# GpSimd's layer-norm rows written as multiply and add, with a newly searched order of the work

## The chip, the cores and the metric

The kernel runs on one core of a Trainium2 chip. The metric is device time in microseconds (us) of one execution; a kernel's time is the median of several runs. The engines are called as in the profile: PE (TensorE matmul), PEld (its weight loads), DVE (VectorE), ACT (ScalarE), POOL (GpSimd) and SP (SyncE, which here only issues DMAs).

## What is computed

One sequence of 2048 rows of width 448 passes through an attention block with 16 heads of width 28 that share one K and one V, and then through a block in which only 8 selected rows take part:

```python
def _layernorm(x, eps=1e-5):
    return (x - mean(x)) / sqrt(var(x) + eps)

def _A_ref(x, wq, wk, wv, wo):             # S=2048, D=448, H=16, Dh=28
    q = (x @ wq) by heads;  k = x @ wk;  v = x @ wv
    p = softmax(q @ k.T * Dh ** -0.5)      # 16 heads x 2048 x 2048
    return (p @ v, heads side by side) @ wo

def _B_ref(x, w_r, w_gate, w_up, w_down):
    r = x @ w_r;  idx = the 8 rows of largest r
    y = (silu(x[idx] @ w_gate) * (x[idx] @ w_up)) @ w_down * sigmoid(r[idx])
    return x, with y added to the rows idx

h  = x + _A_ref(_layernorm(x), wq, wk, wv, wo)
h2 = h + _B_ref(_layernorm(h), w_r, w_gate, w_up, w_down)
```

## The kernel before

**Tiles.** The rows are cut into 16 tiles of 128 (`NT`). Attention goes by 16 blocks of queries (index b, 128 queries of all heads) and in each by 16 tiles of keys (index j). A pair (b, j) is one unit of softmax work, 128 keys against 2048 query columns: PE makes the scores (L804 or L810), another engine makes the exponentials, and PE adds their product with V to one bank of PSUM (L830), which DVE empties at the end of the block (L892).

**Two ways to an exponential.** In 175 of the 256 pairs ACT computes it, in two instructions of 128x1024 each (L846, 350 in all). In the other 81 (`_ND` says how many in each block) DVE turns the scores into the bit pattern of a bf16 power of two, in four instructions (L858, tile `Y0`), and two shifted copies of it are made (`Y1`, and a third, `Y2`), which are weighted together by three products with V. The copy `Y2` is always made by POOL in one instruction of 128x2048 (L874). The copy `Y1` is made either by POOL with L874 again or by DVE in pieces of 128x1536 (L868). `_GK` decides that for three pairs at a time: 1 means POOL, 0 means DVE. With 81 pairs its first 27 entries count.

**The ramp.** Before any of that, a row tile has to be normalised, transposed and projected. `group(g)` (L697) does it for groups of tiles: 0, 1, (2,3), (4,5), (6,7), (8 to 11), (12 to 15). In a group DVE takes mean and variance (L702, L704). For groups 0 to 2 ACT makes the reciprocal deviation (L707, L709); for the four groups from 3 on POOL does it: variance plus epsilon (L712), then the power -0.5 (L714, in tile `rstd`). The normalised rows `of` are then made by DVE for tile 0 (L721), by ACT for tiles 1 and 2 (L726), and by POOL for the 13 tiles 3 to 15, with the row mean subtracted and the result multiplied by `rstd` (L730). PE transposes them (L741), DVE copies the transposes into `xnT` (L746), PE projects them to K and V (L615, a helper for many matmuls), and DVE writes K (L756) and Vs (L765). A key tile can be used by the softmax once its K and V stand. `q_project` makes the queries of a block (DVE, L786).

**After the blocks.** `evict` divides by the softmax's sum with the help of small DMAs and a multiplication on POOL (L901); `out_proj` projects, takes the second layer norm (POOL makes a power of it, L926) and stores the rows; `tail` selects the 8 rows and passes them through the second block.

**The order of the work.** Nothing is ordered by hand. Each instruction is entered with a planned duration and a priority (the third argument of `G.op`, and `prio`), and `_Flow.plan` (L316) simulates the engines with these durations and writes down, for each engine, a fixed order. The chip then runs each engine's list strictly in that order, with semaphores for the dependencies. So a wrong planned duration doesn't change what is computed; it makes an order that was meant for another timing. The priorities are offset by a table `_W` by kind of work (A and D: scores for ACT and for DVE, C: L858, S: L868, P and V: products with V, G: the groups, Q: `q_project`, O: `out_proj`), and further constants steer the planner (`_WIN`, `_HOLD`, `_LATE`, `_LOOK`). Planned durations that the text comes back to: 685 ns for L730, 100 ns for L712, 690 ns for L714, 1976 ns for L874 (`_SHIFT`).

Of the kernel before, what the change touches and what calls it, by code (L numbers as in the profile page):

```python
# [7 lines left out]
ALU = mybir.AluOpType  # L8
AX = mybir.AxisListType
F32 = mybir.dt.float32  # L10
# [6 lines left out]
PE, AC, DV, PO, SP = "pe", "act", "dve", "pool", "sp"  # L17
# [7 lines left out]
class _Graph:  # L25
# [208 lines left out]
_STEP = (0, 43, 85)  # L234
_GAIN = 1.57769262
_NP = 8
_GK = (1, 0, 0, 1, 0, 1, 0, 1, 1, 0, 1, 0, 1, 0, 1, 0, 1, 1, 0, 1, 1, 0, 1, 0, 0, 1, 0, 1, 1, 0, 0, 0, 1, 0, 1, 1,
    1, 1, 1, 1)
_ND = (3, 4, 8, 3, 5, 6, 6, 5, 4, 7, 5, 4, 7, 4, 4, 6)
_W = {"A": -13.681, "D": -10.289, "C": -1.28, "S": 2.404, "P": 0.728, "V": -0.715, "G": -3.802, "Q": -12.936, "O":  # L240
    -29.732, "K": 1.19, "E": -0.647, "F": -0.883, "L": 1.034}
_SHIFT = 1976
_LOOK = 14405.4
_WIN = {PE: 155.3, AC: 3448.9, DV: 40.7, PO: 221.1, SP: 1.0}
_LATE = (2, 40.5)
_MOST = {"A": 1, "D": 2, "M": 3, "T": 9}
_TUNE = {}
_HOLD = {"A": 0.0, "D": 281.9}
_LOW = 0
_NEXT = 12.0  # L250

# [249 lines left out]
def _fast(nc, G, sb, ps, psb, flag, scr, rows, A_x, A_wq, A_wk, A_wv, A_wo, B_w_r, B_w_gate, B_w_up, B_w_down, out):  # L501
    S, D, H = A_x.shape[1], A_x.shape[2], 16
    DH = D // H
    FF = B_w_gate.shape[1]
    NT, CK = S // 128, 112
# [8 lines left out]
    EPS = 1e-5  # L514
# [8 lines left out]
    x_sb = sb("x_sb", [128, NT, D], BF16)  # L523
    of = sb("of", [128, NT, RW], BF16)
    bn6 = sb("bn6", [128, NT, 6], F32)
    mv = sb("mv", [128, NT, 2], F32)
    rstd = sb("rstd", [128, NT], F32)
    nb = sb("nb", [128, NT], F32)
    var = sb("var", [128, NT], F32)
    nhalf = sb("nhalf", [128, 4], F32)  # L530
    xnT = sb("xnT", [128, NCH, S], BF16)
# [13 lines left out]
    Q = sb("Q", [128, 3, 4, 128], BF16)  # L545
    K = sb("K", [128, 2, S], BF16)
    Vs = sb("Vs", [128, NC, NT, 32], BF16)
    P = sb("P", [128, NP, 2, 2, 512], BF16)
# [65 lines left out]
    def mm(o, l, r, start, stop):  # L614
        return lambda e: e.matmul(o() if callable(o) else o, lhsT=l, rhs=r, start=start, stop=stop)  # L615

    def bank(u, p=slice(0, 128), c=slice(0, 512), t=None):
        return lambda: (ps if t is None else t)[p, u.b[0], c]
# [32 lines left out]
    for g in range(2, len(loads)):  # L651
# [3 lines left out]
         writes=["ident"])  # L655
# [6 lines left out]
         writes=["pq0"])  # L662
    G.op(DV, lambda e: e.tensor_single_scalar(pq[:, 1:2], pidx[:, :], 32, ALU.bitwise_and), 62, reads=["pidx"],
         writes=["pq1"])
    G.op(DV, lambda e: e.tensor_scalar(kcol[:, 0:1], pq[:, 1:2], 0, KSCALE, ALU.is_equal, ALU.mult), 62, reads=["pq1"],
         writes=["k0"])
    G.op(DV, lambda e: e.tensor_scalar(kcol[:, 1:2], pq[:, 1:2], 32, KSCALE, ALU.is_equal, ALU.mult), 62,
         reads=["pq1"], writes=["k1"])
    G.op(DV, lambda e: e.tensor_scalar(kcol[:, 4:5], pq[:, 0:1], DH, ZERO / KSCALE, ALU.is_equal, ALU.mult), 62,
         reads=["pq0"], writes=["k4"])  # L670
    for r in range(2):
        G.op(DV, lambda e, r=r: e.tensor_scalar(kcol[:, 2 + r:3 + r], kcol[:, r:r + 1], kcol[:, 4:5], None, ALU.mult), 62,
             reads=["k%d" % r, "k4"], writes=["kb%d" % r])
    G.op(DV, lambda e: e.tensor_single_scalar(qone[:, :], pq[:, 0:1], DH, ALU.is_ge), 62, reads=["pq0"],
         writes=["qone"])
# [6 lines left out]
    for r in range(4):  # L682
        G.op(AC, lambda e, r=r: e.activation(wk_rep[0:CK, :, 32 * r:32 * r + DH], wk_sb[0:CK, :, :], ACT.Identity), 140,
             reads=["wk_sb"], writes=[("wkr", r)], after=[G.last_w["wk_rep"][0]])
# [12 lines left out]
    def group(g):  # L697
        tl_ = groups[g]
        n, t0, t1 = len(tl_), tl_[0], tl_[-1] + 1
        G.prio = (-3000, -2990, -2980)[g] if g < 3 else t0 / 16.0 + W["G"]  # L700
        for t in tl_:
            G.op(DV, lambda e, t=t: e.bn_stats(bn6[:, t, :], x_sb[:, t, :]), 516, reads=[("x", t)], writes=[("bn6", t)],  # L702
                 after=[G.last_w[("xnT", 0)][0]] if t == 2 else [G.last_w[("nb", 3)][0]] if t in (4, 5) else (), prio=-3001 if g == 2 else None)
            G.op(DV, lambda e, t=t: e.bn_aggr(mv[:, t, :], bn6[:, t, :]), 89, reads=[("bn6", t)], writes=[("mv", t)],  # L704
                 prio=-3001 if g == 2 else None)
        if g < XA:
            G.op(AC, lambda e: e.activation(var[:, t0:t1], mv[:, t0:t1, 1], ACT.Ln, bias=ebias[:, 0:1]), 200,  # L707
                 reads=[("mv", t) for t in tl_] + ["ebias"], writes=[("var", g)])
            G.op(AC, lambda e: e.activation(rstd[:, t0:t1], var[:, t0:t1], ACT.Exp, scale=-0.5), 200, reads=[("var", g)],  # L709
                 writes=[("rstd", g)])  # L710
        else:
            G.op(PO, lambda e: e.tensor_scalar(var[:, t0:t1], mv[:, t0:t1, 1], EPS, None, ALU.add), 100,  # L712
                 reads=[("mv", t) for t in tl_], writes=[("var", g)])
            G.op(PO, lambda e: e.tensor_tensor(rstd[:, t0:t1], var[:, t0:t1], nhalf[:, 0:n], ALU.pow), 690,  # L714
                 reads=[("var", g), "nhalf"], writes=[("rstd", g)])
        if 0 < g < XA:
            G.op(DV, lambda e: e.scalar_tensor_tensor(nb[:, t0:t1], mv[:, t0:t1, 0], -1.0, rstd[:, t0:t1], ALU.mult, ALU.mult), 70,
                 reads=[("rstd", g)] + [("mv", t) for t in tl_], writes=[("nb", t) for t in tl_], prio=-3002 if g == 2 else None)
        for t in tl_:
            if g == 0:  # L720
                G.op(DV, lambda e, t=t: e.tensor_scalar(  # L721
                    of[:, t, :].rearrange("p (a b) -> p a b", a=2)[:, :, 0:D // 2], x_sb[:, t, :],
                    mv[:, t, 0:1], rstd[:, t:t + 1], ALU.subtract, ALU.mult), 420,
                     reads=[("x", t), ("mv", t), ("rstd", g)], writes=[("of", t)])
            elif g < XA and t < 3:
                G.op(AC, lambda e, t=t: e.activation(of[:, t, 0:D], x_sb[:, t, :], ACT.Identity, bias=nb[:, t:t + 1],  # L726
                                                     scale=rstd[:, t:t + 1]), 640,
                     reads=[("x", t), ("nb", t), ("rstd", g)], writes=[("of", t)])
            else:
                G.op(PO, lambda e, t=t: e.tensor_scalar(of[:, t, 0:D], x_sb[:, t, :], mv[:, t, 0:1], rstd[:, t:t + 1],  # L730
                                                        ALU.subtract, ALU.mult), 685,
                     reads=[("x", t), ("mv", t), ("rstd", g)], writes=[("of", t)])
        for a in range(t0, t1, 2):
            m = min(2, t1 - a)
            u = G.unit()

            def cut(a, ch):
                return 2 * (ch // 2) if a == 0 else 0

            def tr(k, ch, u=u, a=a, m=m):  # L740
                return lambda e: e.transpose(psb[0:CK, u.b[0], (ch * m + k) * 128:(ch * m + k + 1) * 128],  # L741
                                             of[:, a + k, ch * CK + cut(a, ch):(ch + 1) * CK + cut(a, ch)], ident[:, :])
            G.op(PE, [tr(k, ch) for k in range(m) for ch in range(NCH)], m * 4 * (150 if g == 0 else 80),
                 reads=[("of", a + k) for k in range(m)] + ["ident"], writes=[u.key], take=u)
            dst = xnT[0:CK, :, a * 128:(a + m) * 128]
            G.op(DV, lambda e, u=u, m=m, dst=dst: e.tensor_copy(  # L746
                dst, psb[0:CK, u.b[0], 0:NCH * m * 128].rearrange("p (c n) -> p c n", c=NCH)), 65 + m * 265,
                 reads=[u.key], writes=[("xnT", a + k) for k in range(m)], free=u)
        sl = slice(t0 * 128, t1 * 128)
        w = n * 128  # L750
        uk = G.unit()
        G.op(PE, [mm(bank(uk, c=slice(0, w)), wk_rep[0:CK, ch, :], xnT[0:CK, ch, sl], ch == 0, ch == NCH - 1)
                  for ch in range(NCH)], 4 * (145 if g == 0 else 5 + w / 2.4), reads=[("wkr", r) for r in range(4)] + ["wk_rep"] + [("xnT", t) for t in tl_],
             writes=[uk.key], take=uk)
        for r in range(2):
            G.op(DV, lambda e, r=r: e.tensor_scalar(K[:, r, sl], ps[:, uk.b[0], 0:w], kcol[:, r:r + 1],  # L756
                                                        kcol[:, 2 + r:3 + r], ALU.mult, ALU.add), 190 + w * 1.04,
                     reads=[uk.key, "k%d" % r, "kb%d" % r], writes=[("K", r, t) for t in tl_], free=uk)
        if g == 0:
            q_project(0)  # L760
        uv = G.unit()
        G.op(PE, [mm(bank(uv, c=slice(32 * k, 32 * k + DH)), xnT[0:CK, ch, (t0 + k) * 128:(t0 + k + 1) * 128], wv_sb[0:CK, ch, :],
                     ch == 0, ch == NCH - 1) for k in range(n) for ch in range(NCH)], n * 4 * 55,
             reads=["wv_sb"] + [("xnT", t) for t in tl_], writes=[uv.key], take=uv)
        G.op(DV, lambda e: e.tensor_tensor(  # L765
            Vs[:, :, t0:t1, 1:1 + DH],
            ps[:, uv.b[0], 0:n * 32].rearrange("p (t c) -> p t c", c=32)[:, :, 0:DH].unsqueeze(1).broadcast_to([128, NC, n, DH]),
            vco[:, :, :].unsqueeze(2).broadcast_to([128, NC, n, DH]), ALU.mult), 65 + NC * n * 29,
            reads=[uv.key, "Vs0"] + ["vco%d" % v for v in range(NC)], writes=[("V", t) for t in tl_], free=uv)
# [906 lines left out]
def bass_sequential_preLN__grouped_kv_mqa__moe_arch_mod__prompt_kernel(  # L1676
# [3 lines left out]
    with es:  # L1680
# [11 lines left out]
        def build(cls, fn, pre, *args):  # L1692
# [6 lines left out]
            return g  # L1699

        G = build(_Flow, _fast, "")
        R = build(_Graph, _exact, "x_", G)

# [53 lines left out]
```

## Time and profile before

The median of three runs is 376.84 us (375.97 to 377.87). One execution was profiled; its own time was 377.56 us, of which 375.6 us are the span from its first to its last instruction and about 2 us lie around it.

| stretch of the profiled execution | what happens there |
|---|---|
| 0 to 10 us | loads, constants, tiles 0 and 1 |
| 10 to 49 us | the ramp: tiles 2 to 15 are normalised and projected, while ACT already works on the first pairs |
| 49 to 355 us | softmax on ACT, DVE and POOL together, PE between them |
| 355 to 376 us | last block's projection, selection of 8 rows, second block, scatter |

Over the span PE is busy for 89%, DVE for 90%, ACT for 89% and POOL for 80%. A row of the groups names line, engine, operation and tiles, then the count, the busy time in us, the mean duration in ns, and the idle time of that engine right ahead of it with what ended it. A row of the chain gives start and length in us. A row of the stretches gives the length, then busy time with the number of instructions of each engine, then the clock that PE was granted (1.00 is full), and the DMAs.

### The profile page before, as it was taken

The page shows a single profiled execution, that of the slowest core. Times are in us where ns is not written, and L with a number is a line of the kernel's source. Part 1 is how long each engine was busy: PE and PEld are TensorE (multiplying, and loading weights), DVE is VectorE, ACT ScalarE, POOL GpSimd, SP SyncE. Part 2 cuts the span into 40 slices and gives each one's busy share as a digit, 9 for nine tenths or more (in the row PEclk, how much of TensorE's full clock was granted, in tenths as well). Part 3 has the DMA queues.
Part 4 walks back from the last instruction along what each step waited for, and adds up shares of the span by engine and source line. Part 5 has one row for each costly group of instructions (what it writes and reads, how often), then busy time and mean ns, then how long its engine had stood idle before and what let it go on. Part 6 is the DMA issues. An engine that isn't in the chain of part 4 may idle for free.

```text
span 375.6 us, 8343 instructions
## 1 busy us (share of the span) xinstructions
PE 334.1 (89%) x3417; PEld 110.6 (29%) x3417; DVE 339.8 (90%) x693; ACT 334.7 (89%) x379; POOL 301.4 (80%) x211
## 2 busy tenths in 40 slices
PE   3786798999898999989998999999999989999985
PEld 3432322132323232322232232323232322222234
DVE  7763499899999897999999999999999999999984
ACT  5655399799999999999999999999999999999850
POOL 7799549569949899889789996999999997769701
PEclk9966699799999899999999999999999999999996
DMA  7661000010100010101000010000011060011100
GB/s 189 169 240 46 2 1 2 3 32 25 31 28 29 3 44 13 55 15 45 1 27 31 13 45 27 29 28 31 7 52 35 23 198 31 14 43 29 41 25 9
DMA packets 17974, 16.08 MB, mean 43 GB/s; under 512 B 6303, under 2 KB 15039, under 8 KB 17931
## 3 DMA queue, kind: packets, MB, share of 16 engines
q1 hardware_dynamic: 16426, 14.93, 12.9%
q8 instruction: 28, 0.46, 0.5%
q10 hardware_dynamic: 1392, 0.45, 0.5%
q0 software_dynamic: 112, 0.12, 0.1%
q14 instruction: 16, 0.12, 0.1%
HBM read 11.78 MB, written 3.71 MB: 41 GB/s over the span
## 4 chain that ended last, share of the span: by engine, by line
ACT 65%; DVE 14%; POOL 9%; PE 6%; DMA 3%; issue 1%; POOLq 0%; ACTq 0%; DVEq 0%
ACT P L846 65%; DVE Y L858 6%; POOL of L730 6%; PE ps L615 2%; PE ps L804 2%; DMA Rb<-l_scr 1%; DMA wqx<-in_A_wq_dram 1%; DVE Y L868 1%; PE ps L830 1%; POOL Y L874 1%; POOL rstd L714 1%; DMA l_scr<-Rc 1%; PE ps L741 1%; POOL On L901 1%; DVE junk L932 0%
## 5 line engine op out<-in xcount | busy, mean ns | idle before, releaser
L846 ACT ACTIVATE P<-ps 128x1024 bf16<-128x1024 f32 x350 | 323.3, 1227 | 21.9 <-PE ps L804 19.3
L874 POOL TENSOR_SCALAR Y<-Y 128x2048 int16<-128x2048 int16 x123 | 233.4, 1897 | 41.9 <-DVE Y L858 33.1
L858 DVE TENSOR_SCALAR Y<-ps 128x512 int16<-128x512 f32 x324 | 204.6, 678 | 7.5 <-PE ps L810 4.1
L804 PE MATMUL ps<-Q,K 32*128 32x512 bf16 (+1 forms) x700 | 139.3, 396 | 16.3 <-ACT P L846 13.8
L810 PE MATMUL ps<-Q,K 32*128 32x512 bf16 x324 | 102.6, 388 | 0.2 <-DVE Y L858 0.2
L830 PE MATMUL ps<-Y,Vs 128*32 128x512 bf16 x972 | 87.1, 393 | 1.7 <-DVE Ot L892 0.4
L804 PEld LDWEIGHTS ps<-Q,K 32*128 32x128 bf16 (+1 forms) x700 | 33.1, 92 | 138.5 <-ACT P L846 120.0
L830 PE MATMUL ps<-P,Vs 128*32 128x512 bf16 x700 | 62.4, 391 | 0.1
L868 DVE TENSOR_SCALAR Y<-Y 128x1536 int16<-128x1536 int16 x52 | 48.2, 936 | 0.1
L830 PEld LDWEIGHTS ps<-Y,Vs 128*32 128x32 bf16 x972 | 20.6, 93 | 42.5 <-issue 22.9
L810 PEld LDWEIGHTS ps<-Q,K 32*128 32x128 bf16 x324 | 24.8, 91 | 7.4 <-DVE Y L858 3.6
L730 POOL TENSOR_SCALAR of<-x_sb,mv,rstd 128x448 bf16<-128x448 bf16 x13 | 24.1, 1865 | 1.1 <-ACT rstd L709 0.7
L615 PE MATMUL ps<-xnT,wqx 112*128 112x128 bf16 x256 | 23.2, 232 | 0.4 <-DVE Y L858 0.2
L901 POOL TENSOR_TENSOR On<-Ot,Rb 128x512 bf16<-128x512 f32 x15 | 19.1, 1272 | 4.3 <-DMA Rb<-l_scr 3.3
L741 PE MATMUL ps<-ident,of 128*112 128x128 bf16 x64 | 8.1, 294 | 14.5 <-POOL of L730 9.2
L830 PEld LDWEIGHTS ps<-P,Vs 128*32 128x32 bf16 x700 | 14.5, 94 | 20.8 <-issue 20.0
L615 PE MATMUL ps<-wo_pad,On 128*128 128x448 bf16 x64 | 18.8, 363 | 0.5 <-DVE On L1063 0.3
L615 PEld LDWEIGHTS ps<-xnT,wqx 112*128 112x128 bf16 x256 | 15.9, 103 | 9.8 <-issue 5.7
L746 DVE COPY xnT<-ps 112x1024 bf16<-112x1024 bf16 (+1 forms) x9 | 5.7, 629 | 10.8 <-PE ps L741 10.6
L926 POOL TENSOR_TENSOR st<-st,nhalf 128x1 f32<-128x1 f32 x15 | 8.3, 552 | 5.8 <-DVE st L924 5.3
L756 DVE TENSOR_SCALAR K<-ps,kcol 128x256 bf16<-128x256 f32 (+2 forms) x14 | 7.4, 573 | 5.9 <-PE ps L615 5.8
L786 DVE TENSOR_SCALAR Q<-ps,qone 128x512 bf16<-128x512 f32 (+1 forms) x16 | 11.5, 721 | 0.7 <-PE ps L615 0.7
(162 smaller groups left out, 178.7 us busy)
## 6 DMA issues: line engine op xcount, KB each, us to landing
Rb<-l_scr SPq DMA_DIRECT2D x15, 256.0 KB
out_dram<-of SPq DMA_DIRECT2D x16, 112.0 KB, 2.3
n_rows<-of SPq DMA_DIRECT2D x14, 113.0 KB, 2.2
xnT<-in_B_w_down_dram SPq DMA_DIRECT2D x1, 1568.0 KB, 6.9
x_sb<-in_A_x_dram SPq DMA_DIRECT2D x3, 448.0 KB, 4.2
wg_sb<-in_B_w_gate_dram SPq DMA_DIRECT2D x1, 1344.0 KB, 8.4
wu_sb<-in_B_w_up_dram SPq DMA_DIRECT2D x1, 1344.0 KB, 6.7
wqx<-in_A_wq_dram ACTq DMA_DIRECT2D x1, 392.0 KB, 4.5
```

The lines of the kernel that those rows point to most:

```text
L615: return lambda e: e.matmul(o() if callable(o) else o, lhsT=l, rhs=r, start=start, stop=stop)
L730: G.op(PO, lambda e, t=t: e.tensor_scalar(of[:, t, 0:D], x_sb[:, t, :], mv[:, t, 0:1], rstd[:, t:t + 1], ALU.subtract, ALU.mult), 685, rea ...
L741: return lambda e: e.transpose(psb[0:CK, u.b[0], (ch * m + k) * 128:(ch * m + k + 1) * 128], of[:, a + k, ch * CK + cut(a, ch):(ch + 1) * ...
L786: G.op(DV, lambda e, c=c, src=src: e.tensor_scalar(Q[:, b % 3, c[0]:c[1], :], src(), qone[:, 0:1], None, ALU.add), 60 + n * 150, reads=[u. ...
L804: return e.matmul(ps[:, u.b[q], :], lhsT=K[a:a + w, r, j * 128:(j + 1) * 128], rhs=Q[a:a + w, b % 3, :, :].rearrange("p h n -> p (h n)"), ...
L810: return e.matmul(ps[:, u.b[0], :], lhsT=K[a:a + 32, u.i() % 2, j * 128:(j + 1) * 128], rhs=Q[a:a + 32, b % 3, :, :].rearrange("p h n -> p ...
L830: return e.matmul(ps[32 * i:32 * i + 32, ACC, :], lhsT=Vs[:, v, j, :], rhs=src(i), start=info["first"] == o.idx, stop=info["last"] == o.idx)
L846: G.op(AC, lambda e, u=u: e.activation(P[:, sl, u.r(), :, :], two(u), ACT.Exp, bias=EB, scale=OCT), 916, reads=[("U", "A", b, j, k)], writ ...
L858: G.op(DV, lambda e, u=u, g0=g0: e.tensor_scalar(Y0[:, g0, :].bitcast(I16), ps[:, u.b[0], :], 0.0, TOP - STEP[-1], ALU.max, ALU.min), 599, ...
L868: G.op(DV, lambda e, a12=a12, w=w: e.tensor_scalar(Y1[:, a12:a12 + w, 0:512].bitcast(I16), Y0[:, a12:a12 + w, :].rearrange("p a b -> p (a ...
L874: G.op(PO, lambda e, k=k, yk=yk: e.tensor_scalar(yk.bitcast(I16), Y0[:, 4 * s:4 * s + 4, :].bitcast(I16), 1.0, float(STEP[k]), ALU.mult, A ...
L901: G.op(PO, lambda e: e.tensor_tensor(On[:, rb, :, :].rearrange("p h n -> p (h n)"), Ot[:, rb, :], Rb[:, rb, :], ALU.mult), 1353, reads=[(" ...
```

## The change

POOL's normalised rows are computed as x times `rstd` plus a bias, in place of x minus mean, times `rstd`. The bias `nb` is the negated mean times `rstd`. The negated mean (`nmu`, a new tile) is made by DVE, in one instruction for each of the groups from 3 on; POOL multiplies it by `rstd`. The sum of variance and epsilon goes from POOL to DVE. Tile 3 belongs to group 2, whose bias was already made by DVE (L717) for tile 2; POOL's instruction for tile 3 now reads it. The planned duration of the power becomes 440 + 150 n ns for n tiles; that of the normalised row stays 685 ns. The planner's constants are replaced, and in `_GK` entry 24 goes from 0 to 1 (the other entries that differ are past the 27 that count).

```diff
-_GK = (1, 0, 0, 1, 0, 1, 0, 1, 1, 0, 1, 0, 1, 0, 1, 0, 1, 1, 0, 1, 1, 0, 1, 0, 0, 1, 0, 1, 1, 0, 0, 0, 1, 0, 1, 1,
+_GK = (1, 0, 0, 1, 0, 1, 0, 1, 1, 0, 1, 0, 1, 0, 1, 0, 1, 1, 0, 1, 1, 0, 1, 0, 1, 1, 0, 1, 0, 0, 0, 1, 1, 1, 1, 1,
     1, 1, 1, 1)
-_W = {"A": -13.681, "D": -10.289, "C": -1.28, "S": 2.404, "P": 0.728, "V": -0.715, "G": -3.802, "Q": -12.936, "O":
-    -29.732, "K": 1.19, "E": -0.647, "F": -0.883, "L": 1.034}
+_W = {"A": -4.267, "D": 0.869, "C": -5.23, "S": 11.397, "P": 0.551, "V": -9.818, "G": -3.982, "Q": -12.655, "O":
+    -19.863, "K": 0.879, "E": -0.427, "F": -0.86, "L": 1.09}
-_LOOK = 14405.4
-_WIN = {PE: 155.3, AC: 3448.9, DV: 40.7, PO: 221.1, SP: 1.0}
-_LATE = (2, 40.5)
+_LOOK = 9462.7
+_WIN = {PE: 146.6, AC: 2996.9, DV: 15.5, PO: 432.7, SP: 1.0}
+_LATE = (2, 125.6)
-_HOLD = {"A": 0.0, "D": 281.9}
+_HOLD = {"A": 9.3, "D": 293.6}
...
+    nmu = sb("nmu", [128, NT], F32)
...
-            G.op(PO, lambda e: e.tensor_scalar(var[:, t0:t1], mv[:, t0:t1, 1], EPS, None, ALU.add), 100,
+            G.op(DV, lambda e: e.tensor_scalar(var[:, t0:t1], mv[:, t0:t1, 1], EPS, None, ALU.add), 62,
                  reads=[("mv", t) for t in tl_], writes=[("var", g)])
-            G.op(PO, lambda e: e.tensor_tensor(rstd[:, t0:t1], var[:, t0:t1], nhalf[:, 0:n], ALU.pow), 690,
+            G.op(DV, lambda e: e.tensor_scalar(nmu[:, t0:t1], mv[:, t0:t1, 0], -1.0, None, ALU.mult), 62,
+                 reads=[("mv", t) for t in tl_], writes=[("nmu", g)])
+            G.op(PO, lambda e: e.tensor_tensor(rstd[:, t0:t1], var[:, t0:t1], nhalf[:, 0:n], ALU.pow), 440 + 150 * n,
                  reads=[("var", g), "nhalf"], writes=[("rstd", g)])
+            G.op(PO, lambda e: e.tensor_tensor(nb[:, t0:t1], nmu[:, t0:t1], rstd[:, t0:t1], ALU.mult), 150,
+                 reads=[("rstd", g), ("nmu", g)], writes=[("nb", t) for t in tl_])
...
-                G.op(PO, lambda e, t=t: e.tensor_scalar(of[:, t, 0:D], x_sb[:, t, :], mv[:, t, 0:1], rstd[:, t:t + 1],
-                                                        ALU.subtract, ALU.mult), 685,
-                     reads=[("x", t), ("mv", t), ("rstd", g)], writes=[("of", t)])
+                G.op(PO, lambda e, t=t: e.tensor_scalar(of[:, t, 0:D], x_sb[:, t, :], rstd[:, t:t + 1], nb[:, t:t + 1],
+                                                        ALU.mult, ALU.add), 685,
+                     reads=[("x", t), ("nb", t), ("rstd", g)], writes=[("of", t)])
```

## The prediction

> **What bounds the kernel now.** I read the head of the page first, then its chain, then the busy time by stretches.
>
> ```profile
> span 375.6 us, 8343 instructions
> PE 334.1 (89%) x3417; PEld 110.6 (29%) x3417; DVE 339.8 (90%) x693; ACT 334.7 (89%) x379; POOL 301.4 (80%) x211
> ACT 65%; DVE 14%; POOL 9%; PE 6%; DMA 3%; issue 1%; POOLq 0%; ACTq 0%; DVEq 0%
> ```
>
> Three engines are busy for nine tenths, and the chain lies mostly on ACT. The profiled execution took 377.56 us, 0.72 over the median of 376.84, and 1.96 of it lie outside the span. All sums below are made against the span; I carry the difference over to the median.
>
> The averages hide where the idle tenth is. The stretches show it:
>
> ```profile
> 10.14:20.00 9.86, 8.01 (x85) 5.03 (x82) 7.52 (x22) 6.25 (x7) 7.23 (x8) 1.00 0.65 199
> 20.00:30.00 10.00, 7.04 (x56) 2.87 (x53) 6.69 (x20) 6.16 (x7) 9.31 (x8) 0.66 0.55 188
> 30.00:48.83 18.83, 14.16 (x109) 7.00 (x110) 7.63 (x12) 7.90 (x9) 12.72 (x9) 0.64 0.07 18
> 60.00:80.00 20.00, 18.38 (x181) 4.82 (x177) 18.49 (x30) 18.07 (x21) 12.73 (x7) 0.83 0.05 14
> 80.00:350.00 270.00, 253.33 (x2572) 74.15 (x2568) 262.17 (x501) 268.56 (x294) 234.92 (x139) 0.99 0.11 34
> 350.00:375.60 25.60, 18.49 (x289) 9.97 (x289) 18.67 (x68) 10.42 (x19) 8.74 (x8) 0.85 0.07 19
> ```
>
> The columns are PE, PEld, DVE, ACT, POOL. From 80 to 350 us ACT is idle for 1.4 us of 270: nothing that leaves ACT's list alone can gain there. From 10.14 to 48.83 us, the ramp, ACT works 6.25 + 6.16 + 7.90 = 20.3 of 38.7 us and DVE 7.52 + 6.69 + 7.63 = 21.8. So 18.4 us of ACT and 16.9 us of DVE are lost in the ramp, and only POOL is nearly full. Whatever shortens the ramp moves everything behind it forward, for at most 18.4 us. The waits in the ramp say who was late:
>
> ```profile
> ACT P L846 <- PE ps L804: 18.2, 12, 2.9
> DVE xnT L746 <- PE ps L741: 10.6, 5, 3.0
> PE ps L741 <- POOL of L730: 9.2, 5, 2.2
> DVE K L756 <- PE ps L615: 5.8, 4, 2.8
> ```
>
> Read from below: POOL's normalised rows release PE's transposes, these release DVE's copies, and ACT waits for scores that are queued on PE behind the transposes. The chain in the same stretch (start, length) is almost all POOL:
>
> ```profile
> 13.37 0.24 POOL var L712
> 13.69 0.75 POOL rstd L714
> 14.54 3.73 POOL of L730 x2
> 19.38 3.72 POOL of L730 x2
> 23.23 1.09 PE ps L741 x8
> 26.68 7.39 POOL of L730 x4
> 35.52 7.40 POOL of L730 x4
> 42.96 0.65 PE ps L741 x8
> ```
>
> The twelve rows of groups 3 to 6 lie on it with 3.73 + 3.72 + 7.39 + 7.40 = 22.2 us. This is the stage that the change touches.
>
> **The normalised row.** POOL's groups:
>
> ```profile
> L874 POOL TENSOR_SCALAR Y<-Y 128x2048 int16<-128x2048 int16 x123 | 233.4, 1897 | 41.9 <-DVE Y L858 33.1 <-PE ps L830 0.3
> L730 POOL TENSOR_SCALAR of<-x_sb,mv,rstd 128x448 bf16<-128x448 bf16 x13 | 24.1, 1865 | 1.1 <-ACT rstd L709 0.7
> L926 POOL TENSOR_TENSOR st<-st,nhalf 128x1 f32<-128x1 f32 x15 | 8.3, 552 | 5.8 <-DVE st L924 5.3
> L714 POOL TENSOR_TENSOR rstd<-var,nhalf 128x2 f32<-128x2 f32 (+1 forms) x4 | 3.5, 886 | 0.3
> L692 POOL COPY wqx<-wqx 112x448 bf16<-112x448 bf16 x2 | 1.1, 554 | 0.8 <-DMA wqx<-in_A_wq_dram 0.8
> L712 POOL TENSOR_SCALAR var<-mv 128x2 f32<-128x2 f32 (+1 forms) x4 | 1.0, 240 | 2.7 <-DVE mv L704 2.7
> L1006 POOL MEMSET wg_sb<- 64x896 f32 x1 | 0.8, 837 | 0.1
> L1002 POOL CAST tl<-pidx 128x1 bf16<-128x1 int32 x2 | 0.3, 176 | 0.0
> 51.54 17.72 POOL L874 TENSOR_SCALAR Y<-Y 128x2048 int16<-128x2048 int16 x9 [8.63 <-DVE Y L858]
> ```
>
> The striking pair is the first two. L874, which multiplies and adds, passes 2048 elements a partition in 1897 ns; L730, which subtracts and multiplies, needs 1865 ns for 448. That is 0.93 against 4.2 ns an element, on the same engine with the same instruction. The change gives L730 the operation pair of L874. The ends for the new duration: not below the plain copy of 448 bf16 elements, 554 ns (L692), and not above today's 1865 ns, if the slowness comes from something that stays. In between, take 240 ns (L712, an instruction of almost no elements) as the fixed part: (1897 - 240) / 2048 = 0.81 ns an element, so 240 + 448 x 0.81 = 600 ns. I take 600, because L874 is the only row with the same pair of operations, and 554 lies beside it. What stays is that L730's two scalars are read from tiles, one value a partition, and L874's are constants; also bf16 against int16. No row shows multiply and add with scalars from tiles on POOL, so this is the risk.
>
> Back to back, nine L874 take 17.72 us, (17.72 - 1.90) / 8 = 1.98 from start to start, 0.08 more than one. So a row costs 0.68 us in a sequence and twelve cost 8.2 in place of 22.2: **-14.1 us on POOL's path**. With 1865 ns it would be nothing.
>
> The Trainium skill's GPSIMD Engine Reference, section "Performance versus the Vector engine", has a rule that speaks against the change: a body of at most two operations an element is bound by the port, at 1.03 cycles an element, whichever operations they are; both forms have two. By its 1.2 GHz that would be 0.86 ns an element. L874's 0.93 agrees and L730's 4.2 doesn't; so the rule doesn't hold for every pair, and what breaks it is open. Whether form or operands break it is the first rival.
>
> **The small instructions, once for each of four groups.** Removed from POOL: L712, 0.24 + 0.08 = 0.32 us, 1.3 us in all on the path. Added to POOL: the bias, a product of 128x2 or 128x4. No row shows it; it lies between the cast of one element (176 ns) and the power of one (552 ns, L926). I take 250, near L712, and 0.08 for the gap: +1.3 us, 1.0 to 2.5. Power: unchanged, L714. Added to DVE: variance and negated mean. Their like on DVE:
>
> ```profile
> L924 DVE TENSOR_SCALAR st<-of x15: 140/144/154, 88.7 to 357.4; 128x1 f32<-128x1 f32 x15
> L868 DVE TENSOR_SCALAR Y<-Y 128x1536 int16<-128x1536 int16 x52 | 48.2, 936 | 0.1
> 48.97 9.86 DVE L858 TENSOR_SCALAR Y<-ps 128x512 int16<-128x512 f32 x16
> ```
>
> Eight of 0.14 us are 1.1 us of DVE time, and only the variance, 4 x 0.14 = 0.6 us, is on the path; the negated mean runs while POOL takes the power (0.75 us) and would cost 0.14 a group without that cover. The new waits: POOL's power waits for DVE's variance where L712 waited for DVE's mean, one hand-over as before; the bias waits for the power on its own engine. Behind both stand the normalised rows on POOL, and for these PE's transposes wait. Tile 3's row now waits for DVE's bias as well; its transposes need tile 2 from ACT too, which ends later than a 0.6 us row, so I take nothing for it (at best -1).
>
> The two memsets of 0.84 us (L1006) stand on POOL between groups 4 and 5, where POOL now waits for DVE anyway. With a faster POOL part of that wait goes and they may stick out: 0 to +1.7, I take +0.8.
>
> Sum on the path: -14.1 - 1.3 + 1.3 + 0.6 + 0.8 = **-12.7 us**.
>
> **What is late next in the ramp.** DVE's 21.8 us from 10.14 us on, plus 1.1 new, could end at 33.0 at the earliest, where it starts its first softmax pair at 48.97 now. With -12.7 it ends at about 36.1 and is then 88% busy: possible, and the reason why I don't take more. ACT would keep 18.4 - 12.7 = 5.7 us of idle time in the ramp. PE was granted 0.66 and 0.64 in the last two stretches of the ramp, in which it was busy for 70 and 75%, against 1.00 at 81% in the first and 0.99 at 94% from 80 us on; if the fuller stretches go on carrying the higher clock, that pays for the denser work.
>
> **The new order, and the three pairs that go to POOL.** Entry 24 of the table moves the second copy of three pairs late in the run: DVE loses four L868, 4 x 0.94 = 3.7 us, POOL gets three L874, 5.9 us; POOL is busy for 234.9 of 270 us before 350 and has room. The end:
>
> ```profile
> 330.81 24.48 ACT L846 ACTIVATE P<-ps 128x1024 bf16<-128x1024 f32 x26
> 357.95 0.42 ACT L1056 ACTIVATE Rb<-Ot 128x256 f32<-128x256 f32 x1 [2.66 <-DVE Ot L1054]
> ```
>
> ACT ends its last pair at 355.3 and then waits 2.7 us for DVE, which carries the chain there. DVE relieved by 3.7 us can give back at most these 2.7; ACT's and PE's own last steps need some of it, so I take -0.5 (0 to -2.7). The rest of the new order I cost at nothing: ACT's steady work has 1.4 us of idle time to lose, and both orders are made by one planner from nearly the same durations. What it costs if it is worse is the last rival.
>
> **Forecast: -12.7 - 0.5 = -13.2 us.** Profiled execution 364.4, span 362.4, median 363.6.
>
> **Rivals.**
>
> *The form isn't the reason.* If per-partition scalars or bf16 make L730 slow, the row stays at 1865 ns, the path changes by -1.3 + 1.3 + 0.6 = +0.6 us, less up to 0.5 at the end: 376.9, no change. For it: L874 has neither; the rule above would also make both forms cost the same. Against it: the plain copy L692 passes bf16 in 554 ns, so only scalars are left. Chance 0.10.
>
> *Another queue takes over the ramp.* DVE's waits of 10.6 and 5.8 us are nine round trips to PE, in fixed order on both sides. If about 10 of these 16.4 us stay, since transposes, copies, projections and K of a group still follow one another and scores stand between them, DVE ends its ramp at 43 and not at 36: -5.8 us, 371.0. For it: the trips of a group are serial. Against it: the longest waits sit right behind L730, and the statistics of the coming groups can fill the gaps. Chance 0.16.
>
> *The new order starves ACT in the steady stretch.* From 60 to 80 us ACT lost 1.9 us, in the one stretch behind the ramp in which PE's clock fell, to 0.83 on the mean. An order with more such places pays about 1.9 us for each. It takes seven of them between 50 and 350 us to eat the gain, and eight or more to be slower; with nine: 376.84 - 13.2 + 17.1 = 380.7. For it: the offsets change much (S from 2.4 to 11.4, D from -10.3 to 0.9). Against it: only one such event is in the 300 us now. Chance 0.07.
>
> *More than forecast.* All of ACT's 18.4 us in the ramp would give 358.4; chance of beating 16 us 0.05.
>
> **How the numbers follow.** The forecast's own case (9 to 16 us gained) has 0.62 and spans 360.8 to 367.8. The range runs from 358.4, the bound by ACT's idle time, to 371.8, which takes in the second rival; left out are the first rival, the third, and a little of the second's far side, about 0.2. What a measurement of this kernel can tell from no change is about 0.5%, 1.9 us. Faster by more than that: 0.62 + 0.16 + 0.05 = 0.83, less 0.01 for the far side of the second rival: 0.82. Within it: the first rival and that far side, 0.11. Slower: 0.07.
>
> **What would show it.** The normalised rows at 550 to 700 ns, in 13 instructions; ACT's idle time before L846's successor at 5 to 8 us where the page has 21.9 now; DVE's first softmax pair at about 36 us; PE's clock in the ramp above 0.8; L868 48 times and L874 126 times; ACT from 80 to 335 us as full as now. The forecast is wrong if the rows are still above 1.5 us, or if they are short and DVE's first pair still starts after 41 us, or if ACT's idle time appears again behind the ramp.

## The result, and the profile after

The changed kernel takes 361.58 us (median of four, 360.2 to 365.21) against 377.17; the ratio is 0.9605 with a 95% interval of 0.9529 to 0.968. Forecast were 363.6 us in a range of 358.4 to 371.8. Measured once more on another chip it took 361.76 us, ratio 0.9617 (0.9574 to 0.9659). Medians here are over all executions; the ratios are worked out from undisturbed ones of both kernels and are not quotients of the medians, so the two can differ by some tenths of a per cent.

The page of the changed kernel, its head and the engines of the chain:

```profile
span 359.3 us, 8357 instructions
PE 324.4 (90%) x3417; PEld 108.0 (30%) x3417; DVE 336.7 (94%) x697; ACT 333.7 (93%) x379; POOL 291.7 (81%) x214
ACT 80%; DVE 10%; PE 5%; DMA 2%; issue 1%; POOL 1%; POOLq 0%; ACTq 0%; DVEq 0%
```

ACT and DVE do nearly the same work in a span that is 16.3 us shorter, and POOL's share of the chain falls from 9 to 1%. The line numbers are up to five higher than before: L735 is the normalised row, L851 ACT's exponential, L863 DVE's.

The groups on POOL and DVE that the change touches:

```profile
L735 POOL TENSOR_SCALAR of<-x_sb,rstd,nb 128x448 bf16<-128x448 bf16 x13 | 9.1, 715 | 1.0 <-DVE nb L722 0.6
L879 POOL TENSOR_SCALAR Y<-Y 128x2048 int16<-128x2048 int16 x126 | 239.1, 1897 | 35.4 <-DVE Y L863 25.7 <-DVE of L928 0.7 <-PE ps L835 0.2
L873 DVE TENSOR_SCALAR Y<-Y 128x1536 int16<-128x1536 int16 x48 | 44.6, 935 | 0.1
```

The row fell from 1865 to 715 ns. POOL's list in the ramp (start, length), and DVE's first softmax pair:

```profile
14.03 0.73 POOL L717 TENSOR_TENSOR rstd<-var,nhalf 128x2 f32<-128x2 f32 x1 [3.60 <-DVE nmu L715]
14.85 0.19 POOL L719 TENSOR_TENSOR nb<-nmu,rstd 128x2 f32<-128x2 f32 x1
15.15 1.41 POOL L735 TENSOR_SCALAR of<-x_sb,rstd,nb 128x448 bf16<-128x448 bf16 x2
17.76 1.41 POOL L735 TENSOR_SCALAR of<-x_sb,rstd,nb 128x448 bf16<-128x448 bf16 x2
20.01 0.84 POOL L1011 MEMSET wu_sb<- 64x896 f32 x1
21.50 1.01 POOL L717 TENSOR_TENSOR rstd<-var,nhalf 128x4 f32<-128x4 f32 x1 [0.66 <-DVE nmu L715]
22.89 2.80 POOL L735 TENSOR_SCALAR of<-x_sb,rstd,nb 128x448 bf16<-128x448 bf16 x4
27.21 2.80 POOL L735 TENSOR_SCALAR of<-x_sb,rstd,nb 128x448 bf16<-128x448 bf16 x4
37.97 17.72 POOL L879 TENSOR_SCALAR Y<-Y 128x2048 int16<-128x2048 int16 x9 [7.96 <-DVE Y L863]
```

```profile
35.40 9.74 DVE L863 TENSOR_SCALAR Y<-ps 128x512 int16<-128x512 f32 x16
```

Twelve rows take 1.41 + 1.41 + 2.80 + 2.80 = 8.4 us. The last one ends at 30.0 us, where it ended at 42.9 before, and DVE begins its first pair at 35.4 in place of 49.0. The busy time by stretches (length, then PE, PEld, DVE, ACT, POOL, then PE's clock):

```profile
10.14:20.00 9.86, 9.50 (x112) 5.47 (x112) 9.73 (x32) 7.91 (x9) 5.71 (x10) 1.00 0.70 195
20.00:30.00 10.00, 7.78 (x92) 4.27 (x88) 8.43 (x24) 7.54 (x8) 8.85 (x14) 1.00 0.56 198
30.00:36.00 6.00, 5.35 (x57) 2.23 (x57) 4.44 (x8) 5.14 (x6) 0.01 (x1) 1.00 0.19 55
36.00:60.00 24.00, 22.29 (x226) 6.92 (x223) 24.00 (x40) 23.87 (x27) 18.98 (x10) 1.00 0.02 3
60.00:80.00 20.00, 18.77 (x206) 5.49 (x202) 20.00 (x39) 20.00 (x23) 16.79 (x10) 1.00 0.12 37
80.00:334.00 254.00, 239.96 (x2437) 71.01 (x2437) 246.57 (x469) 253.79 (x277) 227.37 (x135) 1.00 0.11 35
```

In the ramp, now 10.14 to 36 us, ACT is idle for 25.86 - 7.91 - 7.54 - 5.14 = 5.3 us, where it was 18.4. From 10 to 20 us DVE is busy for 9.7 of 9.9 us: it has taken POOL's place as the fullest engine there, and no POOL instruction is left on the chain between 10 and 45 us. PE's clock is 1.00 in every stretch up to the tail.

### The profile page after: what moved, and what is told of

It is laid out like the page before. It is cut to its first block, busy times and chain, and to the rows that moved or that the text cites. A ratio compares the mean times of both kernels' runs of the same rounds, so it can differ in the third digit from the quotient of the medians.

```text
span 359.3 us, 8357 instructions
## 1 busy us (share of the span) xinstructions
PE 324.4 (90%) x3417; PEld 108.0 (30%) x3417; DVE 336.7 (94%) x697; ACT 333.7 (93%) x379; POOL 291.7 (81%) x214
## 4 chain that ended last, share of the span: by engine, by line
ACT 80%; DVE 10%; PE 5%; DMA 2%; issue 1%; POOL 1%; POOLq 0%; ACTq 0%; DVEq 0%
ACT P L851 80%; PE ps L616 2%; DVE Y L863 2%; PE ps L809 1%; DVE bn L703 1%; DMA wqx<-in_A_wq_dram 1%; DVE K L761 1%; DVE Y L873 1%; DMA cidx<-gidx 1%; DVE xnT L751 1%; PE ps L835 1%; POOL wqx L1030 0%; POOL st L931 0%; DVE gidx L1026 0%; DVE Q L791 0%
## 5 line engine op out<-in xcount | busy, mean ns | idle before, releaser
L851 ACT ACTIVATE P<-ps 128x1024 bf16<-128x1024 f32 x350 | 322.2, 1249 | 6.2 <-PE ps L809 6.0
L879 POOL TENSOR_SCALAR Y<-Y 128x2048 int16<-128x2048 int16 x126 | 239.1, 1897 | 35.4 <-DVE Y L863 25.7
L863 DVE TENSOR_SCALAR Y<-ps 128x512 int16<-128x512 f32 x324 | 203.6, 679 | 4.1 <-PE ps L815 3.2
L809 PE MATMUL ps<-Q,K 32*128 32x512 bf16 (+1 forms) x700 | 135.5, 386 | 17.4 <-ACT P L851 13.3
L815 PE MATMUL ps<-Q,K 32*128 32x512 bf16 x324 | 107.8, 384 | 0.6 <-DVE of L952 0.5
L873 DVE TENSOR_SCALAR Y<-Y 128x1536 int16<-128x1536 int16 x48 | 44.6, 935 | 0.1
L815 PEld LDWEIGHTS ps<-Q,K 32*128 32x128 bf16 x324 | 26.3, 91 | 9.6 <-DVE Y L863 5.5
L835 PEld LDWEIGHTS ps<-P,Vs 128*32 128x32 bf16 x700 | 14.7, 94 | 18.6 <-issue 16.6
L616 PEld LDWEIGHTS ps<-xnT,wqx 112*128 112x128 bf16 x256 | 15.3, 101 | 8.7 <-issue 5.9
L927 DVE BATCH_NORM_STATS2 bn<-ps 128x6 f32<-128x448 f32 x15 | 9.3, 622 | 1.8 <-PE ps L616 1.8
L746 PE MATMUL ps<-ident,of 128*112 128x128 bf16 x64 | 5.7, 235 | 5.3 <-DVE of L726 5.3
L897 DVE COPY Ot<-ps 128x512 f32<-128x512 f32 x15 | 10.2, 678 | 0.3 <-PE ps L835 0.3
L616 PE MATMUL ps<-x_sb,ident 128*128 128x448 bf16 x37 | 10.2, 356 | 0.1
L952 DVE TENSOR_SCALAR of<-ps,st 128x448 bf16<-128x448 f32 x14 | 10.3, 734 | 0.0
```

The source lines that it names most:

```text
L809: return e.matmul(ps[:, u.b[q], :], lhsT=K[a:a + w, r, j * 128:(j + 1) * 128], rhs=Q[a:a + w, b % 3, :, :].rearrange("p h n -> p (h n)"), ...
L815: return e.matmul(ps[:, u.b[0], :], lhsT=K[a:a + 32, u.i() % 2, j * 128:(j + 1) * 128], rhs=Q[a:a + 32, b % 3, :, :].rearrange("p h n -> p ...
L835: return e.matmul(ps[32 * i:32 * i + 32, ACC, :], lhsT=Vs[:, v, j, :], rhs=src(i), start=info["first"] == o.idx, stop=info["last"] == o.idx)
L851: G.op(AC, lambda e, u=u: e.activation(P[:, sl, u.r(), :, :], two(u), ACT.Exp, bias=EB, scale=OCT), 916, reads=[("U", "A", b, j, k)], writ ...
L863: G.op(DV, lambda e, u=u, g0=g0: e.tensor_scalar(Y0[:, g0, :].bitcast(I16), ps[:, u.b[0], :], 0.0, TOP - STEP[-1], ALU.max, ALU.min), 599, ...
L873: G.op(DV, lambda e, a12=a12, w=w: e.tensor_scalar(Y1[:, a12:a12 + w, 0:512].bitcast(I16), Y0[:, a12:a12 + w, :].rearrange("p a b -> p (a ...
```

## The experiments

Two theories stand against each other. The form: multiply and add is a fast operation on POOL, subtract and multiply a slow one, and twelve rows in a line are the gain. The order: the newly searched plan is the gain, and the row's part is small or hidden.

**The slow row in the new order.** Only the row's form, operands and their dependence change; each engine's order is that of the changed kernel.

```diff
-  e.tensor_scalar(of[:, t, 0:D], x_sb[:, t, :], rstd[:, t:t + 1], nb[:, t:t + 1], ALU.mult, ALU.add)
+  e.tensor_scalar(of[:, t, 0:D], x_sb[:, t, :], mv[:, t, 0:1], rstd[:, t:t + 1], ALU.subtract, ALU.mult)
```

> The changed kernel with every engine's order kept as it is; only the 13 normalised rows on POOL go back to subtract and multiply (the bias is still made, and not used by them). Theory 'the form of the row': each row goes from 0.715 back to about 1.86 us; twelve rows stand one behind the other in the ramp, 12 x 1.15 = 13.8 us, of which one or two may be hidden: 361.6 + 12 to 14 = 373 to 376 us, DVE's first softmax pair at 47 to 49 us. Rival 'the new order': the rows are slow again but the order was the gain: below 367 us.

Measured: 378.29 us against 376.5, ratio 1.0022 (0.999 to 1.0054). With the slow row the whole of the gain is gone; the new order with its moved small instructions has nothing to show for itself. DVE's first pair starts at 48.96 us, as expected, but the time lies above the expected 373 to 376: some 16 us are lost and not 12 to 14. Two of them stand behind the ramp, in the profiled execution (383.01 us, the longest of the ten):

```profile
60.00:80.00 20.00, 19.05 (x189) 5.28 (x186) 18.34 (x30) 18.07 (x21) 12.73 (x7) 0.83 0.05 13
```

ACT is idle for 1.9 us there, in the same stretch and with the same clock of 0.83 as in the kernel before, though the order of the work is the new one.

**The fast row in the old order.** One line of the kernel before changes, and again no engine's order. The mean is left as it stands, neither negated nor scaled, so this kernel does not compute the layer norm.

```diff
-  e.tensor_scalar(of[:, t, 0:D], x_sb[:, t, :], mv[:, t, 0:1], rstd[:, t:t + 1], ALU.subtract, ALU.mult)
+  e.tensor_scalar(of[:, t, 0:D], x_sb[:, t, :], rstd[:, t:t + 1], mv[:, t, 0:1], ALU.mult, ALU.add)
```

> The kernel before with every engine's order kept as it is; only the 13 rows on POOL become x times rstd plus the row mean as it stands in its tile (so the mean is neither negated nor scaled: the row's value is not the layer norm's; operands are as many and of the same kinds as in the change). Theory 'the form of the row': rows of 0.715 us, twelve of them save 13.8 us on POOL, of which DVE's and PE's fixed order gives back one or two: 377.2 - 12 to 14 = 363 to 365 us. What then remains to 361.6 is the new order with the moved small instructions, 2 to 3 us. Rival 'the new order': above 372 us. Side question: ACT's loss of 1.9 us between 60 and 80 us, with PE's clock at 0.83, should go away if it came from the late ramp, and stay if it lies in the old order.

Measured: 361.84 us, ratio 0.9642 (0.9607 to 0.9677). The row and stretches of this kernel:

```profile
L730 POOL TENSOR_SCALAR of<-x_sb,rstd,mv 128x448 bf16<-128x448 bf16 x13 | 9.1, 716 | 1.3 <-ACT rstd L709 0.8
10.14:20.00 9.86, 9.40 (x116) 5.33 (x112) 9.86 (x29) 8.16 (x9) 6.34 (x10) 1.00 0.62 191
20.00:30.00 10.00, 8.57 (x96) 4.73 (x97) 8.20 (x19) 7.95 (x9) 8.13 (x13) 1.00 0.56 196
30.00:36.00 6.00, 5.97 (x64) 2.18 (x63) 5.39 (x9) 5.99 (x8) 0.00 (x0) 1.00 0.21 55
48.83:60.00 11.17, 11.04 (x105) 2.35 (x103) 10.25 (x16) 9.45 (x11) 6.83 (x4) 0.74 0.02 4
```

One line brings 14.7 us. That is more than the 12 to 14 expected, and the time is level with the changed kernel's 361.58: of the 2 to 3 us that were left for the new order, none shows here. ACT's idle time in the ramp is 25.86 - 8.16 - 7.95 - 5.99 = 3.8 us, less than in the changed kernel. The side question is answered in part: the 1.9 us that ACT lost between 60 and 80 us before are still there, 11.17 - 9.45 = 1.7 us, moved forward with the ramp. So they are not left over from the late ramp. They do not lie in the old order alone either, since the new order with the slow row had them too (above).

**Which part of the form is slow.** The kernel before, with another form of the row in each of the 13 tiles.

```diff
+  3: (x, 0.01, 20.0, subtract, mult)      4: (x, rstd, mv, mult, add)      5: (x, mv, rstd, add, mult)
+  6: (x, rstd, mv, mult, subtract)        7: (x, rstd, None, mult)         8: (x, mv, None, subtract)
+  9: (x, mv, 20.0, subtract, mult)       10: (x, 0.01, rstd, subtract, mult)
+ 11: (x, 0.01, 20.0, add, mult)          12: (x, 20.0, 0.01, mult, add)   13: (x, mv, rstd, subtract, mult)
+ 14: (x, rstd, 0.01, mult, add)          15: (x, 20.0, mv, mult, add)
```

> A probe on the kernel before: each of the 13 rows on POOL takes another form, so the rows' values are not the layer norm's: subtract then multiply, add then multiply, multiply then add, multiply then subtract, one operation alone, and each with its scalars from tiles (one value a partition) or as constants. If the operations decide: multiply then add near 0.7 us whatever the scalars, every form with a subtraction, or with the addition ahead of the multiplication, near 1.86. If the scalars decide: the forms with constants near 0.7 and those with two scalars from tiles near 1.86, which the change's rows already speak against. A form of one operation: no row yet; the plain copy has 0.55. The whole time says nothing here.

The rows in the order of the list, start and length first; L731 is entry 3 and L743 entry 15:

```profile
9.53 1.73 POOL L731 TENSOR_SCALAR of<-x_sb 128x448 bf16<-128x448 bf16 x1 [0.68 <-ACT rstd L709]
14.84 0.72 POOL L732 TENSOR_SCALAR of<-x_sb,rstd,mv 128x448 bf16<-128x448 bf16 x1
15.54 0.72 POOL L733 TENSOR_SCALAR of<-x_sb,mv,rstd 128x448 bf16<-128x448 bf16 x1
18.25 1.88 POOL L734 TENSOR_SCALAR of<-x_sb,rstd,mv 128x448 bf16<-128x448 bf16 x1
20.10 1.41 POOL L735 TENSOR_SCALAR of<-x_sb,rstd 128x448 bf16<-128x448 bf16 x1
24.65 1.42 POOL L736 TENSOR_SCALAR of<-x_sb,mv 128x448 bf16<-128x448 bf16 x1
26.14 1.79 POOL L737 TENSOR_SCALAR of<-x_sb,mv 128x448 bf16<-128x448 bf16 x1
28.03 1.78 POOL L738 TENSOR_SCALAR of<-x_sb,rstd 128x448 bf16<-128x448 bf16 x1
29.88 0.56 POOL L739 TENSOR_SCALAR of<-x_sb 128x448 bf16<-128x448 bf16 x1
31.98 0.56 POOL L740 TENSOR_SCALAR of<-x_sb 128x448 bf16<-128x448 bf16 x1
32.64 1.86 POOL L741 TENSOR_SCALAR of<-x_sb,mv,rstd 128x448 bf16<-128x448 bf16 x1
34.48 0.63 POOL L742 TENSOR_SCALAR of<-x_sb,rstd 128x448 bf16<-128x448 bf16 x1
35.20 0.64 POOL L743 TENSOR_SCALAR of<-x_sb,mv 128x448 bf16<-128x448 bf16 x1
```

Addition and multiplication as a pair are fast in either sequence: 0.56 us with two constants, 0.63 with one scalar from a tile, 0.72 with two. That the addition may stand first was not expected. Every tested form with a subtraction is slow, with constants too (1.73), and so is a multiplication or a subtraction alone (1.41, 1.42). So the operations decide; a scalar from a tile adds 0.05 to 0.09 us. Each form stands here in a single instruction; the 13 rows of the changed kernel bear out the 0.72, those of the kernel before the 1.86.

**The plan told the true durations.** The kernel before, rows slow.

```diff
-  var: 100    pow: 690           row: 685
+  var: 240    pow: 440 + 150*n   row: 1850
```

> The kernel before, rows slow, with the plan told POOL's measured durations: 1850 ns for the row where 685 stood, 240 for variance plus epsilon, 440 + 150 n for the power; all other constants of the plan as before. Theory 'the form of the row': POOL's 22 us of rows stay in the ramp and no order takes them away: 373 to 379 us. Rival 'the wrong planned duration': an order that knows the row gains most of the difference: below 368 us.

Measured: 382.02 us, ratio 1.0187 (1.0118 to 1.0256): 1 to 3% slower than the order that was made with the wrong durations, and above the 373 to 379 us expected. In the ramp the true durations do help: from 10.14 to 48.83 us ACT is idle for 13.7 us, where it was 18.4. More than that is lost behind it:

```profile
48.83:60.00 11.17, 10.61 (x74) 3.21 (x71) 8.98 (x15) 8.71 (x10) 10.36 (x6) 0.51 0.01 1
80.00:334.00 254.00, 235.53 (x2392) 70.16 (x2396) 243.91 (x461) 246.81 (x270) 218.45 (x129) 0.99 0.11 34
```

ACT loses 7.2 us from 80 to 334 us and 2.5 just behind the ramp, with PE's clock at 0.51. The rival falls with these constants: knowing the slow row doesn't recover the difference. Why this order does worse behind the ramp wasn't tested; constants searched anew for the true durations might keep the 5 us of the ramp.

**What the search gave.** The changed code with all planner constants of before:

```diff
-  the new _GK, _W, _LOOK, _WIN, _LATE, _HOLD
+  those of the kernel before
```

> The changed code (multiply and add, bias, variance and negated mean on DVE, the power's planned duration) with all of the planner's constants of before, the table for the second copies too: what the new search gave. Theory 'the form of the row is all of it': 361 to 364 us. Rival 'the search matters too': an order from constants that were searched for other durations loses time, as the true durations did in the kernel before (382.0 against 376.5): 366 us or more.

Measured: 364.26 us, 0.9655 (0.9627 to 0.9684), between the two ranges. Beside the changed kernel on one chip:

> The changed kernel itself, beside the two that follow on one chip, to settle what the new search and the table's entry gave. If both matter: 361 to 362 us, 2 to 4 below the other two. If what was seen between them was the chips and the single executions: all three within 1.5 us of each other.

> The changed code with all planner constants of before, the table's entry too, once more beside the changed kernel: 364 us if the old order's loss of 1.8 us on ACT near 55 us, with PE's clock halved, is there again and the rest is small; 361 to 362 if not.

Measured: 361.76 against 364.15 us; ratios to the kernel before 0.9617 (0.9574 to 0.9659) and 0.9655 (0.962 to 0.969). The medians are 2.7 us apart on two chips and 2.4 on one, in the same direction, but the intervals overlap, and the fast row in the old order (361.84) was no slower than the changed kernel. So a gain of the search isn't shown. The traces have one place where it may come from: between 36 and 60 us ACT is idle for 1.3 to 1.9 us in the four kernels with the old constants and fast rows (this one on both chips, the fast row in the old order, and the last one below), and for 0.1 in the changed kernel, on both chips. PE in the fast row's kernel, then in the changed one, around that place:

```profile
44.00:46.00 2.00, 1.34 (x17) 0.45 (x13) 2.00 (x4) 2.00 (x3) 1.92 (x2) 1.00 0.00 0
46.00:48.00 2.00, 1.49 (x14) 0.39 (x11) 2.00 (x4) 2.00 (x3) 1.91 (x2) 0.96 0.00 0
48.00:50.00 2.00, 1.87 (x12) 0.41 (x9) 1.94 (x4) 2.00 (x3) 1.90 (x1) 0.50 0.00 0
50.00:52.00 2.00, 2.00 (x22) 0.39 (x20) 1.48 (x4) 1.61 (x3) 1.90 (x1) 0.50 0.01 4
```

```profile
48.00:50.00 2.00, 1.56 (x18) 0.40 (x14) 2.00 (x4) 2.00 (x4) 1.92 (x2) 1.00 0.00 0
50.00:52.00 2.00, 1.63 (x17) 0.40 (x13) 2.00 (x4) 2.00 (x4) 1.92 (x2) 1.00 0.00 0
```

In the old order PE is busy for 2.83 of 4 us, its clock halves, and ACT waits for the scores while PE catches up. In the changed kernel its emptiest 4 us there hold 3.19, and the clock stays. The Trainium skill's page "TensorE: Matmul & The Clock Gate", Part 1, has the clock granted by how busy the array was recently, in a window of about 3.4 us. These rows fit that, but no experiment here filled the gap to try it, and the next experiment has an execution in which the share doesn't decide.

**The table's entry.** The changed kernel with entry 24 at 0 again.

```diff
-  _GK[24] = 1
+  _GK[24] = 0
```

> The changed kernel with entry 24 of the table back at 0: DVE makes the second copy of those three pairs again, 4 x 0.94 us, POOL three instructions of 1.90 us less; all other constants as in the change. By the prediction's term DVE carries the end and this costs 0.5 us, at most 2.7: 361.6 to 364.3 us. Rival: the end hangs on the last pair's ACT work and the table is free: no difference from 361.6 beyond 0.5.

> The changed kernel with entry 24 of the table back at 0, once more beside the changed kernel: 0.5 us above it, 2.7 at most, by the prediction's term for the end; 4 above it if the first comparison holds.

Measured: 366.03 us, 0.9695 (0.9651 to 0.9739), and on the common chip 368.48, 0.9691 (0.9636 to 0.9746), with single executions from 362.7 to 371.2. Both medians are above the expected 361.6 to 364.3. This can't be the entry alone: in the traces the instructions of PE, DVE, ACT and POOL follow one another as in the changed kernel up to 300 us, and yet in the first profile ACT is idle for 1.1 us between 80 and 320 us, 0.7 of it from 160 to 200 with PE's clock at 0.96, where the changed kernel loses 0 and 0.25 in its two profiles. The second profile, of the same program, loses 1.9 us between 36 and 60 as well. PE there:

```profile
48.00:50.00 2.00, 1.56 (x14) 0.40 (x14) 2.00 (x4) 2.00 (x3) 1.92 (x2) 1.00 0.00 0
50.00:52.00 2.00, 1.66 (x17) 0.49 (x14) 2.00 (x4) 2.00 (x3) 1.92 (x2) 1.00 0.00 0
52.00:54.00 2.00, 1.90 (x11) 0.24 (x10) 2.00 (x4) 2.00 (x3) 1.92 (x2) 0.51 0.01 4
```

Here the clock halves after 4 us in which PE was busy for 3.22. In the first profile the same 4 us hold 1.48 + 1.64 = 3.12, and the clock stays at 1.00. So neither the order of the work nor the busy share of these 4 us decides by itself whether the clock is lost; what does stays open.

The best executions are 363.3 and 362.7 us against 360.2 and 361.0. The ends of the first profile and of the changed kernel's, ACT's last exponentials with the entry at 0, then at 1:

```profile
336.00 3.77 ACT L851 ACTIVATE P<-ps 128x1024 bf16<-128x1024 f32 x4 [0.19 <-PE ps L809]
```

```profile
337.80 1.02 ACT L851 ACTIVATE P<-ps 128x1024 bf16<-128x1024 f32 x1 [0.16 <-PE ps L809]
```

They end at 339.8 against 338.8, and the spans are 361.0 against 359.3. Of this 1.0 us between ACT's last exponentials nearly all was lost earlier, 0.25 in the ramp and 0.7 from 160 to 200 us, where the order is the same. From there to the end it takes 21.2 against 20.5 us, and 21.6 against 20.5 in the second profiles. So the entry, with the order that follows from it behind 300 us, may be worth about 1 us at the end; why executions with the entry at 0 vary so much more stays open.

**Without the bias product.** By the probe, adding the negated mean and then multiplying is as fast, and the product on POOL can go. Once in the changed kernel, once as the smallest edit of the kernel before:

```diff
+  e.tensor_scalar(of[:, t, 0:D], x_sb[:, t, :], nmu[:, t:t + 1], rstd[:, t:t + 1], ALU.add, ALU.mult)
```

> The changed kernel with the rows of groups 3 to 6 as x plus the negated mean, then times rstd, which passed in 0.72 us in the probe: the bias product on POOL is left out for these groups (0.19 us and a gap of 0.1, four times, between the power and the first row). Theory 'POOL's path in the ramp still counts': -1.2 us at most, 360.4. Rival 'DVE fills the ramp now' (9.7 of 9.9 us from 10 to 20 us): no change beyond 0.5 us. An unlucky order, since the planner makes a new one from constants that were searched with the bias product in place: up to 366.

> The kernel before with the smallest edit that makes the rows fast and keeps what is computed: DVE makes the negated mean, the rows are x plus that, then times rstd; variance plus epsilon stays on POOL, no bias product, all planner constants of before. Against the fast rows in the old order (361.8): the same, 361 to 364 us, if the form is all of it; 366 or more if the new order that the planner makes here doesn't fit its constants.

Measured: 365.3 us, 0.9654 (0.9607 to 0.9701), and 362.88 us, 0.9643 (0.9609 to 0.9677). The first is not the 360.4 of its theory; its profiled execution, too, loses 1.9 us of ACT between 36 and 60 us, with PE's clock at 0.86. A kernel with another instruction list gets another order, so what the product itself costs isn't told apart from what that order costs. The second computes the whole kernel with the old constants and comes within 1.3 us of the changed kernel, inside its interval: the search isn't needed for the gain. No version here is clearly better than the changed kernel.

## Why the prediction was right

**The row.** Forecast 600 ns, measured 715; start to start 0.70 (2.80 / 4), where I had 0.68. Twelve: -13.8 us where -14.1 stood. The duration was too short because L874's scalars are constants, and two from tiles cost 0.16 us, as the probe shows; the 0.08 us that I added as a gap don't follow this row, and by luck made up for half of that. The first rival, that scalars or bf16 make the row slow, is refuted: 0.72 with both.

**Which forms are fast.** The Trainium skill's GPSIMD Engine Reference, section "Performance versus the Vector engine", bounds a body of at most two operations by the port, at 1.03 cycles an element. By its 1.2 GHz this gives an estimate of 0.38 us for 448 elements. Addition with multiplication took 0.56, and from these 448 elements to L874's 2048 (int16) the time grows by (1897 - 560) / 1600 = 0.84 ns an element, close to the rule's 0.86. None of the other forms in the probe keeps to it: a single multiplication, by the rule no dearer, took 1.41 us. Why these forms are slow no run here shows.

**The small instructions.** The bias took 0.19 to 0.20 us and a gap of 0.1 (I took 0.33 in all), variance and negated mean on DVE 0.15 each in most groups (0.26 once). The memsets cost nothing (+0.8 stood): POOL waits 0.66 us for DVE behind them. POOL's last row moved by 42.92 - 30.01 = 12.9 us; 12.7 was the sum.

**What is late next.** DVE's first pair at 35.4 (forecast 36.1), ACT's idle time in the ramp 5.3 us (5.7). DVE is the fullest engine from 10 to 20 us. Of the second rival, its round trips to PE, 0.6 us are left for the transposes and 2.4 for K, 3.0 in place of 16.4. This part was right to within a microsecond.

**What the sum lacked.** The gain is 15.3 us by the medians (376.84 - 361.58) and 16.3 by the spans, where 13.2 stood. ACT's time shows where the rest lies (us; the ramp ends at 48.83 in the kernel before and at 36 in the others):

| | before | fast row, old order | changed |
|---|---|---|---|
| ACT idle in the ramp | 18.4 | 3.8 | 5.3 |
| ACT idle from there to its last exponential | 3.37 | 2.23 | 0.94 |
| ACT busy in all | 334.75 | 333.80 | 333.68 |
| last exponential to last instruction | 20.3 | 20.2 | 20.5 |
| span | 375.6 | 358.7 | 359.3 |

The changed kernel gains 13.1 us in the ramp, 2.4 behind it and 1.1 of ACT's busy time, and loses 0.2 at the end: 16.4 by these rows, 16.3 by the spans. The 2.4 and the 1.1 were not in my sum. The busy time is less because isolated exponentials take 1.02 us each where a run of 21 takes 0.92, and fewer are isolated now. That comes with the row, since the fast row in the old order has it too. The idle time behind the ramp is less there as well, by 1.1 us.

**The order, costed at nothing.** The two columns on the right differ by no more than single executions do: what the new order loses in the ramp, 1.5 us, it gains behind it, 1.3. With slow rows it gives nothing (378.29), with fast ones at most 2.4 us, by intervals that overlap. So the term is borne out as far as these runs tell. But the reason that I gave for the last rival was misread: "only one such event" overlooks a second stretch of the kernel before in which PE's clock fell to 0.83 and ACT lost 0.8 us:

```profile
120.00:130.00 10.00, 9.16 (x72) 2.13 (x72) 8.91 (x18) 9.24 (x11) 8.05 (x6) 0.83 0.02 3
```

**The end, "-0.5".** From ACT's last exponential to the last instruction it is 20.5 us now and was 20.3, so the term doesn't show against the kernel before. Against the changed kernel with the entry at 0 (21.2 and 21.6) it may be there.

## What to carry to other kernels

Look at the duration of an instruction per element beside others of the same kind on the same engine: a factor of four between two pairs of operations was visible on the page before any experiment. On POOL write a scale and shift as multiply and add, or add and multiply, even where it costs an extra small instruction for a negated operand; here, at 448 elements a partition, that took a row from 1.86 to 0.72 us. And change the row first, alone, in the order that stands: that brought 14.7 us by itself. A search for a new order belongs behind it; here it was worth a sixth of that at most, and no gain of it is shown.

## What the runs showed of the hardware

On POOL, 448 bf16 elements a partition cost 0.56 us for addition and multiplication with constants and 0.72 with two scalars from tiles, 1.41 for a multiplication alone and 1.42 for a subtraction alone, 1.73 for subtract and multiply with constants, 1.88 for multiply and subtract with two scalars from tiles.

PE's clock halved in one execution after 4 us in which PE was busy for 3.22, and stayed full in another of the same program with 3.12 at the same place.

Six executions of the changed kernel on one chip took 361.0 to 365.08 us, the shortest with a mean granted clock of PE of 0.986, the longest with 0.966. A difference of 2 us between two orders is of that size, and six executions of each did not settle it.
